# Loads of the last stage begun in the stage before it, and one gradient's stores issued by GpSimd, in a spectral layer's training step

## The chip, the cores and the metric

The kernel runs on one core of one Trainium2 chip. A core has TensorE (PE, matrix products), VectorE (DVE) and ScalarE (ACT) for elementwise work, GpSimd (POOL), and SyncE (SP), which in this kernel issues nearly every DMA. A DMA issued by any engine is moved by the core's 16 DMA engines. The metric is device time in microseconds (us), the median of several executions.

## The reference, cut to what matters

The program computes a conditioned layer (a spectral filter, then a dense pair with a squared relu) and all its gradients. With S = 2048 rows, D = 512 columns and F = 1792 hidden columns, all in bf16:

```
sa, ca, ga, sb, cb, gb = rows of silu(c) @ w_mod
h  = layernorm(x) * (1 + ca) + sa
x1 = x + ga * irfft2( rfft2(h) * (w_r + i w_i) )
h2 = layernorm(x1) * (1 + cb) + sb
out = x1 + gb * ( relu(h2 @ w1 + b1)**2 @ w2 + b2 )
outputs: out, then the gradients of sum(out * grad_out) by
         x, w_r, w_i, w1, b1, w2, b2, c, w_mod
```

out_0 is `out`, out_1 the gradient of x, out_2 and out_3 those of w_r and w_i (the spectral filter), out_4 of w1, out_5 of b1, out_6 of w2, out_7 of b2, out_8 of c, out_9 of w_mod.

## The kernel before, in words

The Fourier transforms are products with small cosine and sine matrices. Rows are held 128 to a tile column, 16 such row tiles (t = 0 to 15); the spectrum is held in eight groups (gi = 0 to 7) of 128 x 2 x 2 x 258.

The program goes forward (to about 130 us), through the dense pair forward and back (to about 282 us), and then has two stages that the change touches.

**The middle stage of the way back** (some 282 to 348 us, L1025 to L1135). `spec_f23` (L294) transforms the gradient of the spectral output, group by group: psB on PE (L318), two ACT copies into AE (L324, L325), psC on PE (L306), two ACT copies into G (L308), then `ew_b` (L1117): eight DVE products (L413 to L416) that give the gradient spectrum Z and the filter gradient gW, and the stores of gW to out_2 and out_3 (L1123; six stores for group 0, four for each other). `after_b` (L1125) follows each group: it loads later groups (`load`, L1107: LF from L1109, Z from L1110, X from L1112), loads LG (L1129), fills PE with units of the gradient of w1 (`grad_w1`, L1077, 16 products of 448 columns each, L1081, copied by ACT at L1085 and stored at L1087), and after every second group emits one row of the gradient of w_mod (`GMod.emit`, L447: a broadcast on PE at L452, an ACT copy into the single buffer gmbc at L454, then two wmc loads, L458, four DVE products with sums, L465, four scalings, L462 and L464, two stores, L467). Right after the second unit of `grad_w1` stands `grad_b1` (L1039), whose ACT copy b4 (L1047) is stored to out_5 (L1048). The units, grad_b1 and the broadcast of `emit` take their PSUM from one pool, `mmps`, of two buffers named "mm" in turn.

**The last stage** (some 348 us to the end). `spec_g1` (L331) transforms Z back over one axis (psG, L341, copied out by DVE at L346 and ACT at L348). Then `row_pair` (L1217) goes through the rows two tiles at a time: PE (L370, L380), an ACT copy (L1226), and some 15 DVE operations on the rows n1 and gxl, which `load_rows3` (L1167) loads two pairs ahead from HBM (L1170, L1171); L1231 is the first that reads n1, L1242 the one that reads gxl. Between the pairs PE is filled with 14 units of the gradient of w2 (`grad_w2`, L1147: 16 products of 512 columns, L1150, scaled by DVE at L1153, stored at L1154). A unit needs the whole output gradient g_sb (128 x 16 x 512, loaded at L1173) and one transposed chunk hn of the hidden activations (`load_hn`, L1141, a transposing DMA at L1145). Four hn buffers are loaded before the stage's work, four more in a pool `endp` that comes free when the units of grad_w1 end, and then in turn. `grad_b2` (L1157) and its second half (L1057 to L1065) stand among them.

**What sets the order.** A scheduler orders each engine's instructions by the order of the program text and by priorities when the program is built; on the chip each engine runs its own list strictly in order, SP's list of DMAs too, and waits where an operand, a buffer or a DMA's completion slot is not ready. DMAs from one issuing engine use eight completion slots in turn, so that an issue also waits for the one eight before it. A pool that is allocated over memory of a released pool waits for the last users of that memory: before the change, g_sb's pool `gwp` lies where the LF tiles and the tiles of `spec_f23` lay, so its load waits for the last stores of gW.

Of the kernel before, what the change touches and what calls it, by code (L numbers as in the profile page):

```python
# [12 lines left out]
BF16 = mybir.dt.bfloat16  # L13
# [5 lines left out]
D = 512  # L19
DF = 257  # L20
FP = 258
F = 1792
NFC = 14
NT = 16
# [3 lines left out]
P = 128  # L28
# [15 lines left out]
def w_parts(rows, gi):  # L44

    v = rows.rearrange("(q h g) f -> q h g f", h=2, g=16)
    if gi > 0:
        return [(0, 64, v[:, :, gi, :]), (64, 64, v[:, ::-1, 16 - gi, :])]
    c = rows.rearrange("(q c g) f -> q c g f", c=4, g=16)
    return [(0, 64, v[:, :, 0, :]), (64, 32, c[:, 0:2, 8, :]), (96, 32, c[:, 3:1:-1, 8, :])]  # L50
# [15 lines left out]
def build_basic(tc, constp):  # L66
    nc = tc.nc
    K = {}
    ident = constp.tile([P, P], BF16, name="ident")
    make_identity(nc, ident)  # L70
    K["ident"] = ident
    for nm, shape, dt, val in (("ones_sq", [P, P], BF16, 1.0), ("ones_col", [P, 1], BF16, 1.0), ("ones_q", [P, 32], BF16, 0.0), ("onef", [P, 1], FP32, 1.0),
                               ("nhalf", [P, 4], FP32, -0.5), ("npi", [P, 1], FP32, -math.pi), ("eps", [P, 1], FP32, 1e-5)):
        tl = constp.tile(shape, dt, name=nm)
        nc.vector.memset(tl, val)
        K[nm] = tl
    nc.vector.memset(K["ones_q"][:, 0:1], 1.0)
    pid = constp.tile([P, 1], I32, name="pid")
    nc.gpsimd.iota(pid, pattern=[[0, 1]], base=0, channel_multiplier=1)
    K["pid"] = pid  # L80
    pidf = constp.tile([P, 1], FP32, name="pidf")
    nc.vector.tensor_copy(pidf, pid)
    K["pidf"] = pidf
    return K
# [324 lines left out]
def cmul(nc, pool, A, B, outr, outi, conj_a):  # L409

    p1 = pool.tile([P, 2, 2, FP], BF16, name="p1")
    p2 = pool.tile([P, 2, 2, FP], BF16, name="p2")
    nc.vector.tensor_tensor(p1[:, :, :, 0:DF], A[:, :, :, 0:DF], B[:, :, :, 0:DF], op=ALU.mult)  # L413
    nc.vector.tensor_tensor(p2[:, :, :, 0:DF], A[:, :, :, 0:DF], B[:, :, ::-1, 0:DF], op=ALU.mult)  # L414
    nc.vector.tensor_tensor(outr, p1[:, :, 0, 0:DF], p1[:, :, 1, 0:DF], op=(ALU.add if conj_a else ALU.subtract))
    nc.vector.tensor_tensor(outi, p2[:, :, 0, 0:DF], p2[:, :, 1, 0:DF], op=(ALU.subtract if conj_a else ALU.add))  # L416
# [54 lines left out]
def kernel(  # L471
# [5 lines left out]
    nc = tc.nc  # L477
# [6 lines left out]
    xs_dram = dram.tile([P, 8, 2, 2, FP], BF16, name="xs_dram")  # L484
    h_dram = dram.tile([NFC, P, NT * P], BF16, name="h_dram")
# [6 lines left out]
    g_view = grad_out.rearrange("b (p t) d -> p (b t) d", t=NT)  # L492
# [20 lines left out]
    K = build_basic(tc, constp)  # L513
# [175 lines left out]
    with Priority(tc, LATE):  # L689
        for b in range(NB):  # L690
            for fc in range(NFC):
                ps = mmps.tile([P, SB], FP32, name="mm")
# [331 lines left out]


    gm = GMod(tc, K, scf, gsc, wm_view, out9_view)
    lf2 = tc.alloc_tile_pool(name="lf2", bufs=1, side="right")
    K["LF"] += [lf2.tile([P, 2, 3, P], BF16, name=f"LFb{gi}") for gi in range(4, 8)]
    W4 = 448
    NFB = F // W4  # L1030
    gwa = tc.alloc_tile_pool(name="gwa", bufs=1)
# [7 lines left out]
    def grad_b1():  # L1039

        ps = mmps.tile([P, SB], FP32, name="mm")
        for t in range(NT):
            for fb in range(NFB):
                nc.tensor.matmul(ps[32 * fb:32 * fb + 32, 0:W4], lhsT=K["ones_q"], rhs=ghn[t // 4][:, t % 4, fb * W4:(fb + 1) * W4],
                                 start=(t == 0), stop=(t == NT - 1), tile_position=(0, 32 * fb))
        b4 = gwa.tile([P, W4], BF16, name="b4", bufs=1)
        nc.scalar.copy(out=b4, in_=ps[:, 0:W4])  # L1047
        nc.sync.dma_start(out_5.rearrange("(q f) -> q f", q=NFB), b4[0:P:32, :])  # L1048

    def add_quadrants(ps, pool, out, scale=None):  # L1050
        w = ps.shape[-1]
# [38 lines left out]
    for fp in range(0, NFB, 2):  # L1090
        for dc in range(4):
            for fb in (fp, fp + 1):
                units.append(lambda fb=fb, dc=dc: grad_w1(fb, dc))
    units[1:2] = [lambda w1=units[1]: (w1(), grad_b1())]

    def fill_w1(n):
        for _ in range(n):
            if units:
                units.pop(0)()
# [4 lines left out]
    with tc.tile_pool(name="f23b", bufs=2) as fr, tc.tile_pool(name="ewb", bufs=2) as ew:  # L1104
        Xt = {}

        def load(gi):  # L1107
            if gi >= 4:
                nc.sync.dma_start(K["LF"][gi], LF_dram[:, 2 * gi:2 * gi + 2])  # L1109
            nc.sync.dma_start(Z[gi], wz_dram[:, gi])  # L1110
            Xt[gi] = fr.tile([P, 2, 2, FP], BF16, name="Xb", bufs=4)
            nc.sync.dma_start(Xt[gi], xs_dram[:, gi])  # L1112

        for gi in range(4):
            load(gi)

        def ew_b(gi, G):  # L1117
            cmul(nc, ew, Z[gi], G, Z[gi][:, :, 0, 0:DF], Z[gi][:, :, 1, 0:DF], True)
            gW = ew.tile([P, 2, 2, FP], BF16, name="gW", bufs=3)
            cmul(nc, ew, Xt[gi], G, gW[:, 0, :, 0:DF], gW[:, 1, :, 0:DF], True)  # L1120
            for i, o in enumerate((out_2, out_3)):
                for p0_, n, rows_ in w_parts(o, gi):
                    nc.sync.dma_start(rows_, gW[p0_:p0_ + n, i, :, 0:DF])  # L1123

        def after_b(gi):  # L1125
            if gi + 4 < 8:
                load(gi + 4)
            if gi == 4:
                nc.sync.dma_start(K["LG"], LG_dram)  # L1129
            fill_w1(2 if 0 < gi < 6 else 1)  # L1130
            if gi % 2 == 1:
                gms.pop(0)()

        spec_f23(tc, K, UT, AEs, None, lambda gi: gwa.tile([P, 2, 2, FP], BF16, name="G", bufs=2), ew_b, after_b)
    lf2.release()  # L1135
    gwp = tc.alloc_tile_pool(name="gwp", bufs=1, side="right")
    g_sb = gwp.tile([P, NT, D], BF16, name="g_sb")

    hns, endp = [], {}

    def load_hn():  # L1141
        fc = len(hns)
        if fc < NFC:
            hns.append(endp.get("hn", gwp).tile([P, NT, P], BF16, name="hn", bufs=4))
            nc.sync.dma_start(hns[fc], h_dram[fc, :, :], transpose=True)  # L1145

    def grad_w2(fc):  # L1147
        ps = mmps.tile([P, SB], FP32, name="mm")
        for t in range(NT):
            nc.tensor.matmul(ps, lhsT=hns[fc][:, t, :], rhs=g_sb[:, t, :], start=(t == 0), stop=(t == NT - 1))  # L1150
        gw = gwp.tile([P, D], BF16, name="gw", bufs=3)
        with tc.high_priority():
            nc.vector.tensor_tensor(gw, ps, modb[:, GB_B, :], op=ALU.mult)  # L1153
        nc.sync.dma_start(out6_view[:, fc, :], gw)  # L1154
        load_hn()
# [11 lines left out]
    def load_rows3(t):  # L1167
        if t < NT:
            rows3[t] = (fin.tile([P, 2, D], BF16, name="n1"), fin.tile([P, 2, D], BF16, name="gxl"))
            nc.sync.dma_start(rows3[t][0], n1_dram[:, t:t + 2, :])  # L1170
            nc.sync.dma_start(rows3[t][1], gx1_dram[:, t:t + 2, :])  # L1171

    nc.sync.dma_start(g_sb, g_view)  # L1173
    load_hn()
    load_rows3(0)
    load_rows3(2)
    for _ in range(3):
        load_hn()

    CS = utcs.tile([P, NT, 4, 16, 8], BF16, name="utcs")  # L1180
    spec_g1(tc, K, Z, CS)
# [100 lines left out]
    fp.release()  # L1282
    fin.release()
    gwp.release()
    h2p.release()
    cdp.release()
    cfp.release()
# [35 lines left out]
```

## Time and profile before

| what | value |
|---|---|
| median of 11 runs | 432.09 us (430.2 to 433.57) |
| the profiled execution | 435.41 us, of which its span (first to last instruction) is 433.6 us |
| granted TensorE clock, mean | 0.992 of full speed |
| busy share of the span | PE 92%, DVE 81%, ACT 60%, POOL 3% |
| 282 to 348 us: PE, DVE, ACT busy of 66 us | 63.13, 47.43, 35.02 us; DMA share 0.77, 228 GB/s |
| 348 to 432 us: PE, DVE, ACT busy of 84 us | 74.73, 70.49, 38.49 us; DMA share 0.99, 241 GB/s |
| gW stores (L1123) | 34 on SP, 591 ns to issue and 3.5 us to landing at the median |
| hn loads (L1145) | 14 on SP, 2905 ns to issue and 5.6 us to landing at the median |

How to read it: times are microseconds from the start of the span unless they are marked ns. "PE mm L1150" is TensorE's work at line 1150 that writes the tile "mm"; "SPq" is SP issuing a DMA; "n<-n_dram" is the tile n1 loaded from the tensor n1_dram, as buffer numbers are left out of names. A wait is named with the engine and line that waited, the arrow, and what ended the wait. The DMA share is the mean busy share of the 16 DMA engines. The chain that ended last is followed back from the last instruction, at each step to what released it.

### The profile page before, as it was taken

The numbers are of one execution on the slowest core, as the hardware profiler recorded it, in microseconds if no ns is written. First come the engines' busy times: TensorE is split into PE (matmuls) and PEld (weight loads), VectorE is DVE, ScalarE is ACT, GpSimd is POOL, SyncE is SP. The second block draws the span as 40 slices with busy tenths as digits, with TensorE's granted clock in tenths as the row PEclk, the third lists the DMA queues.
The fourth block names the chain that finished last, engine by engine and source line by source line (L and its number), as shares of the span: only waits on it lengthen the run. The fifth ranks groups of instructions, "written<-read, shape, count | busy, mean of one in ns | idle before, by whom it ended". The sixth has DMA issues, their size and how long they took to land.

```text
span 433.6 us, 7049 instructions
## 1 busy us (share of the span) xinstructions
PE 400.6 (92%) x2375; PEld 195.8 (45%) x2375; DVE 351.1 (81%) x846; ACT 261.2 (60%) x493; POOL 13.0 (3%) x64
## 2 busy tenths in 40 slices
PE   2798999999999999999999999999999799993996
PEld 0344456654434444444444344455565464441332
DVE  6797758958997588978897998929576968977996
ACT  4697889768882188248635855474348375445231
POOL 6210000000000000000000000000000000000000
PEclk9998999999999999999999999999999999999899
DMA  8995789989298569767965997987995699999994
GB/s 238 248 296 144 189 323 275 256 312 219 89 375 260 155 112 322 197 168 201 278 179 172 214 320 251 270 251 223 259 305 154 167 261 274 224 260 237 246 242 160
DMA packets 149738, 101.09 MB, mean 233 GB/s; under 512 B 98753, under 2 KB 135494, under 8 KB 149062
## 3 DMA queue, kind: packets, MB, share of 16 engines
q1 hardware_dynamic: 149138, 100.12, 86.1%
q10 hardware_dynamic: 564, 0.53, 0.4%
q8 instruction: 18, 0.29, 0.3%
q14 instruction: 18, 0.15, 0.1%
HBM read 35.44 MB, written 41.60 MB: 178 GB/s over the span
## 4 chain that ended last, share of the span: by engine, by line
PE 35%; DVE 31%; DMA 13%; ACT 10%; SPq 5%; issue 5%; POOL 1%; ACTq 0%; DVEq 0%
PE og L880 10%; PE mm L853 6%; PE mm L694 5%; PE mm L1150 4%; DMA n<-n_dram 3%; DVE gm_junk L465 3%; DMA x<-in_A_x_dram 2%; DMA LGb<-LG_dram 2%; PE psG L341 2%; PE mod_ps L595 2%; SPq L1145 2%; DVE l_st L795 1%; DVE jk L1235 1%; DMA gh_dram<-gab 1%; DVE p L414 1%
## 5 line engine op out<-in xcount | busy, mean ns | idle before, releaser
L694 PE MATMUL mm<-gT,w2T 128*128 128x512 bf16 x224 | 59.3, 390 | 2.7 <-DVE gab L697 2.3
L1150 PE MATMUL mm<-g_sb,hn 128*128 128x512 bf16 x224 | 51.7, 385 | 4.3 <-DVE gw L1153 4.3
L853 PE MATMUL mm<-h2T,w 128*128 128x512 bf16 x224 | 53.6, 379 | 1.5 <-ACT r L855 1.3
L880 PE MATMUL og<-w1T,gab 128*128 128x512 bf16 x224 | 50.9, 379 | 0.8 <-DVE o L945 0.7
L1081 PE MATMUL mm<-gab,h_sb 128*128 128x448 bf16 x256 | 51.4, 352 | 0.1
L880 PE MATMUL og<-w,h 128*128 128x512 bf16 x224 | 50.3, 379 | 0.0
L855 ACT ACTIVATE r<-mm,b1col 128x512 bf16<-128x512 f32 x56 | 37.0, 685 | 6.1 <-PE mm L853 3.7
L1150 PEld LDWEIGHTS <-hn 128*128 128x128 bf16 x224 | 21.3, 99 | 30.5 <-issue 7.6
L853 PEld LDWEIGHTS <-w 128*128 128x128 bf16 x224 | 21.1, 97 | 30.6 <-issue 8.8
L1081 PEld LDWEIGHTS <-h_sb 128*128 128x128 bf16 x256 | 24.6, 98 | 21.6 <-issue 1.0
L880 PEld LDWEIGHTS <-h 128*128 128x128 bf16 x224 | 21.8, 98 | 26.1 <-issue 1.0
L880 PEld LDWEIGHTS <-gab 128*128 128x128 bf16 x224 | 21.6, 98 | 25.9 <-issue 1.4
L694 PEld LDWEIGHTS <-w2T 128*128 128x128 bf16 x224 | 21.2, 100 | 23.5 <-issue 7.4
L893 ACT CAST G<-og 128x512 bf16<-128x512 f32 x16 | 9.2, 581 | 27.8 <-PE og L880 27.8
L699 ACT CAST gab<-mm 128x512 bf16<-128x512 f32 x36 | 21.7, 604 | 4.5 <-PE mm L694 4.4
L857 DVE TENSOR_TENSOR h<-r 128x1024 bf16<-128x1024 bf16 x28 | 19.1, 683 | 4.9 <-ACT r L855 4.9
L1230 ACT ACTIVATE gs<-gn,inv 128x512 bf16<-128x512 bf16 x16 | 11.4, 716 | 18.1 <-DVE gn L1228 18.1
L1085 ACT CAST gw<-mm 128x448 bf16<-128x448 f32 x16 | 8.7, 543 | 21.4 <-DMA out_dram<-gw 11.5
L413 DVE TENSOR_TENSOR p<-Z,G 128x1028 bf16<-128x1028 bf16 x8 | 5.6, 696 | 17.7 <-ACT G L308 9.4
L697 DVE CAST gab<-mm 128x512 bf16<-128x512 f32 x20 | 13.7, 686 | 7.5 <-PE mm L694 7.4
L372 ACT ACTIVATE Tsb<-psT 128x512 bf16<-128x512 f32 x32 | 18.5, 604 | 1.6 <-PE psT L370 1.6
L465 DVE SCALAR_TENSOR_TENSOR gm_junk<-wmc,onef,gmbc 128x512 bf16<-128x512 bf16 x24 | 17.9, 744 | 1.6 <-ACT gmbc L454 0.7
(287 smaller groups left out, 756.4 us busy)
## 6 DMA issues: line engine op xcount, KB each, us to landing
h_dram<-h SPq DMA_DIRECT2D x28, 256.0 KB, 3.2
gh_dram<-gab SPq DMA_DIRECT2D x28, 256.0 KB, 3.5
w<-in_B_w_dram SPq DMA_DIRECT2D x2, 1792.0 KB, 7.6
wmc<-in_w_mod_dram SPq DMA_DIRECT2D x12, 256.0 KB, 4.4
out_dram<-gwm SPq DMA_DIRECT2D x12, 256.0 KB, 3.4
wz_dram<-Z SPq DMA_DIRECT2D x8, 258.0 KB, 2.4
xs_dram<-Xs SPq DMA_DIRECT2D x8, 258.0 KB, 3.6
Z<-wz_dram SPq DMA_DIRECT2D x8, 258.0 KB, 4.2
```

Of the source, the lines that this page charges most:

```text
L372: nc.scalar.activation(Tsb, ps, AF.Copy, scale=EF_S)
L465: nc.vector.scalar_tensor_tensor(out=junk, in0=wmc[:, i, :], scalar=K["onef"], in1=gmbc, op0=ALU.mult, op1=ALU.mult, accum_out=self.gsc[:, ...
L694: nc.tensor.matmul(ps, lhsT=w2T[:, dc, fc * P:(fc + 1) * P], rhs=gT[b][:, :, dc, :], start=(dc == 0), stop=(dc == 3))
L697: nc.vector.tensor_copy(out=gaT[b][:, fc, :], in_=ps)
L699: nc.scalar.copy(out=gaT[b][:, fc, :], in_=ps)
L853: nc.tensor.matmul(ps, lhsT=w1[:, dc, (fc + i) * P:(fc + i + 1) * P], rhs=h2T[b][:, :, dc, :], start=(dc == 0), stop=(dc == 3))
L855: nc.scalar.activation(r[:, i, :], ps, AF.Relu, bias=b1col[:, fc + i:fc + i + 1])
L857: nc.vector.tensor_tensor(h2, r, r, op=ALU.mult)
L880: nc.tensor.matmul(ps, lhsT=lhs(fc), rhs=rhs[:, fc, :], start=(fc == 0), stop=(fc == NFC - 1))
L1081: nc.tensor.matmul(ps[:, 0:W4], lhsT=h2_sb[:, t, dc * P:(dc + 1) * P], rhs=ghn[t // 4][:, t % 4, fs], start=(t == 0), stop=(t == NT - 1))
L1150: nc.tensor.matmul(ps, lhsT=hns[fc][:, t, :], rhs=g_sb[:, t, :], start=(t == 0), stop=(t == NT - 1))
L1230: nc.scalar.activation(gs[:, i, :], gn[:, i, :], AF.Copy, scale=inv1[:, t + i:t + i + 1], accum_out=rr[:, i, 0:1])
```

## The change

Three things change, all from L1026 on.

- g_sb and two hn buffers move into a pool of their own, `gsp`, which is allocated ahead of the LF tiles, so that it overlaps nothing of the middle stage. g_sb's load is issued in `after_b` of group 4, behind LG; hn 0 and hn 1 are issued in `after_b` of groups 4 and 5, each not ahead of the last X load. At the start of the last stage only hn 2 and hn 3 are loaded, from a `gwp` that now has two hn buffers.
- The stores of gW (34) and of b4 (one) are issued by GpSimd's queue instead of SP's.
- b4 of grad_b1 has no buffer of its own any more: it is written into the pool's one buffer "gmbc", which `GMod.emit` uses next.

In the built program, the order on PE and on DVE is the same as before. On ACT the first half of a copy into AE (L324) now stands before the first gmbc copy, and the second half (L325) directly behind it. On SP, the LF loads of groups 4 to 7, which stood ahead of the first Z, stand behind the first four pairs of Z and X. On GpSimd's queue stand, in order: six gW stores of group 0, four of group 1, the store of out_5, then four for each of groups 2 to 7. hn 2 waits for the last eight of these to land, and the loads of n1 and gxl follow it on SP.

The diff, cut to its core:

```diff
     gm = GMod(tc, K, scf, gsc, wm_view, out9_view)
+    gsp = tc.alloc_tile_pool(name="gsp", bufs=1, side="right")
+    g_sb = gsp.tile([P, NT, D], BF16, name="g_sb")
+    hns, endp = [], {}
+
+    def load_hn():
+        fc = len(hns)
+        if fc < NFC:
+            pool = gsp if fc < 2 else endp.get("hn", endp["gw"])
+            hns.append(pool.tile([P, NT, P], BF16, name="hn", bufs=4 if "hn" in endp else 2))
+            nc.sync.dma_start(hns[fc], h_dram[fc, :, :], transpose=True)
...
-        b4 = gwa.tile([P, W4], BF16, name="b4", bufs=1)
-        nc.scalar.copy(out=b4, in_=ps[:, 0:W4])
-        nc.sync.dma_start(out_5.rearrange("(q f) -> q f", q=NFB), b4[0:P:32, :])
+        b4 = gwa.tile([P, D], BF16, name="gmbc", bufs=1)
+        nc.scalar.copy(out=b4[:, 0:W4], in_=ps[:, 0:W4])
+        nc.gpsimd.dma_start(out_5.rearrange("(q f) -> q f", q=NFB), b4[0:P:32, 0:W4])
...
             Xt[gi] = fr.tile([P, 2, 2, FP], BF16, name="Xb", bufs=4)
-            nc.sync.dma_start(Xt[gi], xs_dram[:, gi])
+            K["Xt"] = nc.sync.dma_start(Xt[gi], xs_dram[:, gi]).ins
...
                 for p0_, n, rows_ in w_parts(o, gi):
-                    nc.sync.dma_start(rows_, gW[p0_:p0_ + n, i, :, 0:DF])
+                    nc.gpsimd.dma_start(rows_, gW[p0_:p0_ + n, i, :, 0:DF])
...
             if gi == 4:
                 nc.sync.dma_start(K["LG"], LG_dram)
+                nc.sync.dma_start(g_sb, g_view)
+            if 4 <= gi < 6:
+                with tc.issue_after(K["Xt"]):
+                    load_hn()
             fill_w1(2 if 0 < gi < 6 else 1)
...
     gwp = tc.alloc_tile_pool(name="gwp", bufs=1, side="right")
-    g_sb = gwp.tile([P, NT, D], BF16, name="g_sb")
-
-    hns, endp = [], {}
-
-    def load_hn():
-        fc = len(hns)
-        if fc < NFC:
-            hns.append(endp.get("hn", gwp).tile([P, NT, P], BF16, name="hn", bufs=4))
-            nc.sync.dma_start(hns[fc], h_dram[fc, :, :], transpose=True)
+
+    endp["gw"] = gwp
...
-    nc.sync.dma_start(g_sb, g_view)
     load_hn()
     load_rows3(0)
     load_rows3(2)
-    for _ in range(3):
-        load_hn()
+    load_hn()
```

More of the change, by code (lines that the diff above doesn't have):

```diff
@@ L1284 @@
     gwp.release()
+    gsp.release()
     h2p.release()
```

## The prediction

> **What bounds the kernel now.** I read the slices of the page first. PE shows 9 in nearly every slice of the whole way back (from 282 us on), so a microsecond is won only where PE stands still, and lost only where it is made to. Then I asked what PE waited for from 280 us to the end (line, releaser, us in total, times, longest):
>
> ```profile
> PE mm L1150 <- DVE gw L1153: 4.3, 1, 4.3
> PE mm L1060 <- DVE gn L1239: 2.6, 1, 2.6
> PE psG L341 <- DVE utcs L346: 2.1, 1, 2.1
> PE mm L1277 <- DVE gcb L1275: 0.5, 1, 0.5
> PE psB L318 <- ACT AE L325: 0.3, 1, 0.3
> ```
>
> Nothing else is over 0.3. The table of 4 us stretches places the first two (PE, PEld, DVE, ACT, POOL busy, then clock, DMA share, GB/s); the clock falls once, behind the second wait:
>
> ```profile
> 392.00:396.00 4.00, 1.52 (x13) 0.64 (x14) 4.00 (x12) 2.43 (x5) 0.00 (x0) 1.00 1.24 247
> 396.00:400.00 4.00, 0.28 (x5) 0.16 (x3) 1.75 (x4) 2.67 (x7) 0.00 (x0) 1.00 0.83 198
> 400.00:404.00 4.00, 3.46 (x10) 0.96 (x10) 4.00 (x12) 1.36 (x3) 0.00 (x0) 0.57 1.09 313
> ```
>
> Behind both stands DVE, and behind DVE the n1 rows of the last stage. From DVE's waits (from 345 us on):
>
> ```profile
> DVE q L1231 <- DMA n<-n_dram: 6.0, 3, 2.3
> ```
>
> From the chain that ended last (start, length):
>
> ```profile
> 385.50 3.69 DMA n<-n_dram
> 394.63 4.54 DMA n<-n_dram
> ```
>
> And from SP's timeline (start, length of the issue):
>
> ```profile
> 348.71 7.01 SPq L1145 DMA_TRANSPOSE hn<-h_dram  x1
> 380.18 5.22 SPq L1145 DMA_TRANSPOSE hn<-h_dram  x2
> 389.96 4.57 SPq L1145 DMA_TRANSPOSE hn<-h_dram  x1
> ```
>
> The reader is to see that each n1 load is issued in the very microsecond in which a transposed h load lets go of SP (355.7, 385.4, 394.5). The transposes are slow to issue (7.0 us at worst, 2.0 at best, median 2.9) since the DMA engines are full: their share is 0.99 of the stretch 348 to 432, and 0.77 of 282 to 348.
>
> **Part 1, the moved loads.** g_sb (2048 KB) and two of 14 hn loads go from 348-366 to some 308-325. DVE's three waits for n1 (1.5, 2.3, 2.3 us) should go: n1 of the first rows then has one transpose ahead of it in place of g_sb and a 7 us one; at 380-395 the engines have less to carry. g_sb's 2 MB at 241 GB/s (that stretch's rate) is 8.5 us of them, the two hn some 4 us each (estimate: landing 4.8 to 10.6, partly overlapped), 16 of 83 busy us. PE order and DVE order are the same instruction for instruction in both programs, so the waits can be followed one by one. L1060 waits behind DVE work that comes 1.5 + 2.3 = 3.8 us sooner: the wait of 2.6 goes. L1150 is then reached 2.6 sooner, at 393.7, and its releaser, gw L1153 (399.8 to 400.5), 6.1 sooner, at 394.4: 0.7 of 4.3 is left, 3.6 are won. The clock's dip goes with it: four matmuls took 1.87 where four take 0.9 warm, and the next dozen 3.04 in place of 2.76: 1.3. What is late next is gw L1153 itself; from 404 PE has no idle time but the last 0.5. **Part 1: 2.6 + 3.6 + 1.3 = 7.5 won.** If the n1 loads stay late it is nothing; never more than the 6.9 of idle plus 1.3, so 0 to 8.2.
>
> What these loads do in the middle stage: SP issues LFb4 to 7 behind the first four Z and Xb pairs instead of before (their first reader, psC of group 4, comes at 314.7); LGb moves from 313.5 to about 303; hn0 (about 319) and hn1 (about 323) come ahead of two wmc loads that DVE wants at 332.3, with 4.2 us landing. A full set of DMA engines there (0.77 x 66 = 51 busy us, 67 with the guests) could make wmc late and so group 6's products and psG's wait of 2.1 longer. Against that, ACT's L1085 waited 6.4 us at 325.7 for a store that stood behind SP's other work and now goes out at about 316; DVE's group 5 began late for it (328.5). Bounds: 2.1 won to 3 lost (a wmc landing as late as the worst Xb, 6.8, behind a slow hn1). I take 0.4 won.
>
> **Part 2, the stores on GpSimd's queue.** SP loses 34 gW issues of 0.6 us and the b4 store: 21 us of SP time, none of it on PE's path, so free by itself. But POOL has them in order, and there is a new wait. grad_b1's b4 now shares the one gmbc buffer, so ACT's first gmbc copy (L454) must wait until out_5 has landed, and out_5 stands on POOL behind all ten stores of groups 0 and 1. Behind that copy on ACT are the second half of AE, two gwm scalings, G and gw1. And PE waits for it: the two "mm" buffers rotate, so the second of the two grad_w1 units begun at 300.40 writes the buffer that this copy empties. Today:
>
> ```profile
> 299.26 0.59 ACT L454 CAST gmbc<-mm 128x512 bf16<-128x512 f32 x1
> 300.40 6.21 PE L1081 MATMUL mm<-gab,h_sb 128*128 128x448 bf16 x32
> 296.17 4.05 SPq L1123 DMA_DIRECT2D out_dram<-gW  x6
> 301.26 2.50 SPq L1123 DMA_DIRECT2D out_dram<-gW  x4
> 305.46 0.64 SPq L1048 DMA_DIRECT2D out_dram<-b  x1
> ```
>
> That second unit begins at 300.40 + 6.21/2 = 303.5. The stores can begin when DVE has group 0's gW, at 296.1; 0.7 sooner, since Xb (which DVE waited for, 8.4 us) follows an out_0 store that took 3.64 beside LFb loads and 2.4 at the median. With c us per store on POOL, out_5 is issued at 295.4 + 10c, lands 3.0 later (the 32-row gW stores' median), and the copy takes 0.6: PE stands from 303.5 to 299.0 + 10c, that is **10c - 4.5 us**. c is shown nowhere: no DMA of this kernel is issued by POOL. From below, SP's own 0.6 for the same store gives 1.5 us; from above, POOL's longest instruction, 128x4 at L401 (1064 ns), 6.1, and a third more (c = 1.4, since ten stores may bring waits for earlier ones' landing) 9.5. A c under 0.45 would cost nothing; a gain is excluded, as out_5 has no reader. I take 0.9: it is the same kind of instruction as SP's row, on the engine of the other, and I lean to the engine: 4.5 us. A gap of that size came with the dip above (1.3) once, gaps of 2.1 and 2.6 did not; I count half, 0.7. **Part 2: 5.2 lost**, 1.5 to 10.8 at the ends.
>
> A rule bears on c. The Trainium skill, "DMA: Bandwidth & Descriptors" (section "Latency and other measured facts"), gives GpSimd's path about 1 us to the first byte, where SP's has 0.6; taken as c, that would make the stall 5.5 and the sum 1.0 worse. No run shown here has it. It speaks against the change, as does a trap in "SBUF — State Buffer" (section "SBUF: two separate sides"): VectorE in a two-port mode keeps GpSimd from writing its descriptors; no row here can show that.
>
> At the seam both effects meet: hn2 and all n1 loads wait for the last gW stores. DVE has gW of group 7 at 343.2; eight stores from 339.1 at 0.9 end at 346.4, landed by 349.4. SP then needs 2.9 for hn2 and n1 4.0: 356.3. It is wanted at 358.8, so free up to c = 1.2.
>
> **Sum.** 7.5 + 0.4 - 5.2 = 2.7 us won. The profiled execution took 435.41 (span 433.6), 0.8% over the median of 432.09, so I subtract from the median: **429.4 us**.
>
> **Rivals.**
> 1. *The new wait wins.* One mechanism, one place: ACT at L454, price 10c - 4.5 + 1.3, against 7.9 won; it decides from c = 1.11. At c = 1.4 it is 10.8 - 7.9 = 2.9 lost: 435.0. For: ten stores in a row in front of one tiny store. Against: SP does them in 0.6. Chance 0.27.
> 2. *The tail keeps its waits.* n1 of rows 10 still stands behind hn8 on SP, and the crowded middle costs 1 or 2: say 3 won in all and 5.2 lost, 434.3. For: the order on SP there is the same pair as before. Against: hn8's buffer is free from 382.5, so only full DMA engines hold it up. Chance 0.13.
> 3. *GpSimd issues as fast as SP* (c = 0.6): 7.9 - 1.5 = 6.4 won, 425.7. For: 34 stores of few bytes. Against: POOL's 1064 ns for four columns. Chance 0.15.
> 4. *It does not do what it says*: the stores stay SP's bound and the seam is as late as before (gW of group 7 is made at 343.2 in either program). Then only the two hn's time is won, 3 to 4, against 5: within 2 of today. Contained in the first two.
> The forecast, with c from 0.75 to 1.05, has 0.45; a small part of it, and of case 2, lies within 0.2% (0.9 us, about what a measurement of this kernel can tell from no change): 0.11 in all. So faster 0.49, slower 0.40. As both signs hold much, the forecast's own range is 427.0 to 431.5. The whole: case 3 with the largest gains (432.1 - 8.2 - 2.1 + 1.5 = 423.3) to case 1 with a crowded middle (432.1 - 7.5 + 3 + 10.8 = 438.4); cut by the ends that need two extremes at once, 424.5 to 438.
>
> **What would show it.** Right: SP's n1 loads follow hn issues of 3 us or less, DVE's L1231 has no wait left, PE no idle 4 us near 390; ACT waits for a DMA at its first gmbc copy near 300, PE at 303.5 for ACT, 3 to 6 us, and POOL's eleven stores show c. Wrong: no wait at that copy (out_5 landed by 303), a clock dip near 305-310 with over 7 us of it, DVE waiting for wmc or n1, or psG's wait grown past 3 us.

## The result and the profile after

The changed kernel takes 438.14 us (median of 12 runs, 436.35 to 440.13) where the kernel before took 432.49 beside it: a ratio of 1.0132 (95% interval 1.0108 to 1.0156), 5.65 us slower. The forecast was 429.4. The profiled execution has a span of 436.7 us and a mean clock of 0.988.

Lines have moved: the matmuls of the gradient of w1 are L1092 (L1081 before), their copy and store L1096 and L1098 (L1085, L1087), the row sums of the gradient of b1 and their copy and store L1055, L1058 and L1059, the gW stores L1134, the hn loads L1036, the matmuls of the gradient of w2 and their scaling L1158 and L1161 (L1150, L1153). What PE waits for from 280 us to the end (line, releaser, us in total, times, longest):

```profile
PE mm L1092 <- ACT gmbc L454: 7.8, 1, 7.8
PE psG L341 <- DVE utcs L346: 2.3, 1, 2.3
PE mm L1158 <- DVE gw L1161: 1.4, 1, 1.4
PE mm L1283 <- DVE gcb L1281: 0.5, 1, 0.5
PE psF L354 <- DVE Z L415: 0.5, 1, 0.5
```

The wait of 2.6 at the row work is gone and that of 4.3 at the gradient of w2 is down to 1.4; a new one of 7.8 stands at the place that the prediction named. The same table of stretches as before (PE, PEld, DVE, ACT, POOL busy, clock, DMA share, GB/s):

```profile
300.00:304.00 4.00, 2.28 (x13) 1.08 (x11) 0.00 (x0) 0.00 (x0) 1.77 (x3) 1.00 1.07 323
304.00:308.00 4.00, 0.00 (x0) 0.00 (x0) 0.00 (x0) 0.00 (x0) 0.00 (x0) 0.56 0.99 400
308.00:312.00 4.00, 1.95 (x6) 0.82 (x6) 1.97 (x7) 2.59 (x5) 0.00 (x0) 0.50 0.11 46
...
400.00:404.00 4.00, 3.40 (x23) 1.39 (x22) 4.00 (x11) 1.39 (x4) 0.00 (x0) 1.00 1.00 230
```

From 304 to 308 no engine computes at all while the DMA engines move 400 GB/s, and the clock is at half (0.56, then 0.50) until 312. The stretch that had a clock of 0.57 before (400 to 404) keeps it whole. Who holds PE is read along three timelines (start, length, what, and in brackets the idle time before it and who ended it). GpSimd's:

```profile
294.57 4.67 POOL L1134 DMA_DIRECT2D out_dram<-gW  x8 [40.80 <-PE mm L1055]
300.99 1.17 POOL L1134 DMA_DIRECT2D out_dram<-gW  x2 [1.76 <-DMA out_dram<-gW]
302.15 0.60 POOL L1059 DMA_DIRECT2D out_dram<-gmbc  x1
```

ACT's, then PE's:

```profile
309.41 0.59 ACT L454 CAST gmbc<-mm 128x512 bf16<-128x512 f32 x1 [10.20 <-DMA out_dram<-gmbc]
```

```profile
299.10 3.19 PE L1092 MATMUL mm<-gab,h_sb 128*128 128x448 bf16 x16
310.05 5.49 PE L1092 MATMUL mm<-gab,h_sb 128*128 128x448 bf16 x16 [7.76 <-ACT gmbc L454]
```

Eight gW stores go out in 4.67 us, 0.58 each; the ninth then waits 1.76 for a completion slot, that is for the first of them to land; out_5 is issued at 302.15 and lands 7.2 us later. PE's next unit takes 5.49 us where a warm one takes 3.19: another 2.3. Just ahead of out_5, SP had issued LG (1.5 MB), which it issued at 313.52 in the kernel before:

```profile
300.11 0.99 SPq L1140 DMA_DIRECT2D LGb<-LG_dram  x1
```

In the last stage the moved loads did what they were to do. SP's timeline shows hn 0 and hn 1 in the middle stage, with an out_4 store between them, and n1 behind one short hn:

```profile
326.52 6.17 SPq L1036 DMA_TRANSPOSE hn<-h_dram  x1
332.79 0.53 SPq L1098 DMA_DIRECT2D out_dram<-gw  x1
333.37 5.12 SPq L1036 DMA_TRANSPOSE hn<-h_dram  x1
338.54 1.10 SPq L458 DMA_DIRECT2D wmc<-in_w_mod_dram  x2
...
358.77 1.89 SPq L1036 DMA_TRANSPOSE hn<-h_dram  x1
360.71 0.58 SPq L1178 DMA_DIRECT2D n<-n_dram  x1
```

No wait of DVE for n1 is left. DVE's waits of the middle stage show what the two transposes did instead, ahead of wmc:

```profile
DVE gm_junk L465 <- DMA wmc<-in_w_mod_dram: 4.1, 1, 4.1
```

**Three marks on PE** split the way back so that single runs can be compared: the first matmul of the row sums (the start of "L1044" below), before which PE has the same work in every version; the first matmul of the gradient of w2, with which the last stage's fill begins; and the last matmul. From the views of these lines (count, ns at least/at the median/at most, first and last start in us), before and after:

```profile
L1044 PE MATMUL mm<-gab,ones_q x64: 352/352/363, 292.5 to 295.3; 128*32 128x448 bf16 x64
L1150 PE MATMUL mm<-g_sb,hn x224: 379/379/631, 361.0 to 429.2; 128*128 128x512 bf16 x112
L1277 PE MATMUL mm<-ident,gcb x1: 218/218/218, 430.1 to 430.1; 128*4 128x128 bf16 x1
```

```profile
L1055 PE MATMUL mm<-gab,ones_q x64: 352/352/363, 291.2 to 294.0; 128*32 128x448 bf16 x64
L1158 PE MATMUL mm<-g_sb,hn x224: 376/379/390, 371.0 to 432.5; 128*128 128x512 bf16 x112
L1283 PE MATMUL mm<-ident,gcb x1: 218/218/218, 433.4 to 433.4; 128*4 128x128 bf16 x1
```

So the **middle** took 361.0 - 292.5 = 68.5 us and takes 79.8; the **tail** took 69.1 and takes 62.4. 6.7 won, 11.3 lost (7.8 in which PE stands idle, 2.3 of clock, 0.7 more at psG and psF): 4.6 slower in the two profiled executions, 5.65 in the medians. The first mark itself lies between 290.8 and 293.9 in the profiles of this study, so a single profile says nothing finer than some 1.5 us about a total.

### The profile page after: what moved, and what is told of

The parts are those of the page before. It is cut to its first block, busy times and chain, and to the rows that moved or that the text cites. A ratio compares the mean times of both kernels' runs of the same rounds, so it can differ in the third digit from the quotient of the medians.

```text
span 436.7 us, 7064 instructions
## 1 busy us (share of the span) xinstructions
PE 399.5 (91%) x2375; PEld 195.0 (45%) x2375; DVE 351.0 (80%) x846; ACT 261.0 (60%) x493; POOL 33.5 (8%) x99
## 4 chain that ended last, share of the span: by engine, by line
PE 45%; DVE 25%; ACT 11%; DMA 9%; issue 4%; SPq 3%; POOL 1%; ACTq 0%; DVEq 0%; POOLq 0%
PE og L880 11%; PE mm L853 9%; PE mm L694 5%; PE mm L1092 4%; PE mm L1158 3%; PE psG L341 3%; SPq L1036 3%; DVE gm_junk L465 3%; DMA out_dram<-gW 2%; PE mod_ps L595 2%; DMA out_dram<-gmbc 2%; DMA n_dram<-x_sb 2%; ACT AE L324 1%; DVE gw L1161 1%; DMA out_dram<-gx 1%
## 5 line engine op out<-in xcount | busy, mean ns | idle before, releaser
L1092 PE MATMUL mm<-gab,h_sb 128*128 128x448 bf16 x256 | 53.7, 363 | 7.8 <-ACT gmbc L454 7.8
L694 PE MATMUL mm<-gT,w2T 128*128 128x512 bf16 x224 | 57.2, 379 | 3.2 <-DVE gab L697 2.6
L1158 PE MATMUL mm<-g_sb,hn 128*128 128x512 bf16 x224 | 50.5, 379 | 1.4 <-DVE gw L1161 1.4
L1092 PEld LDWEIGHTS <-h_sb 128*128 128x128 bf16 x256 | 25.2, 100 | 30.9 <-issue 11.5
L1158 PEld LDWEIGHTS <-hn 128*128 128x128 bf16 x224 | 21.1, 98 | 27.2 <-issue 3.8
L1134 POOL DMA_DIRECT2D out_dram<-gW x34 | 19.9, 598 | 81.3 <-PE mm L1055 40.8
L1096 ACT CAST gw<-mm 128x448 bf16<-128x448 f32 x16 | 8.6, 540 | 20.8 <-PE mm L1092 14.1
L861 DVE TENSOR_TENSOR gab<-r,gab 128x1024 bf16<-128x1024 bf16 x28 | 19.1, 681 | 0.0
```

The costliest lines, as they stand in the source:

```text
L694: nc.tensor.matmul(ps, lhsT=w2T[:, dc, fc * P:(fc + 1) * P], rhs=gT[b][:, :, dc, :], start=(dc == 0), stop=(dc == 3))
L861: K["gh"] = nc.vector.tensor_tensor(gh, r, gh, op=ALU.mult).ins
L1092: nc.tensor.matmul(ps[:, 0:W4], lhsT=h2_sb[:, t, dc * P:(dc + 1) * P], rhs=ghn[t // 4][:, t % 4, fs], start=(t == 0), stop=(t == NT - 1))
L1134: nc.gpsimd.dma_start(rows_, gW[p0_:p0_ + n, i, :, 0:DF])
```

## The experiments

Theory 1: the buffer that b4 shares with gmbc is the loss, and the moved loads win what was forecast. Theory 2: the moved loads crowd the middle stage, and the stand is only where that shows. All runs, by the ratio to the kernel before (95% interval) and, from one profile each, middle and tail as above:

| run | what it is | ratio | middle | tail |
|---|---|---|---|---|
| | before | 1 | 68.5 | 69.1 |
| | the change | 1.0132 (1.0108 to 1.0156) | 79.8 | 62.4 |
| e3 | stores on GpSimd alone | 0.9983 (0.9949 to 1.0017) | 66.6 | 69.9 |
| e4 | moved loads alone | 1.0048 (1.0012 to 1.0083) | 73.6 | 65.0 |
| e5 | shared buffer alone | 1.0111 (1.0068 to 1.0154) | 74.4 | 69.4 |
| e1 | the change, own b4 | 0.9937 (0.9893 to 0.9982) | 70.7 | 62.4 |
| e2 | the change, out_5 on SP | 1.0032 (0.9999 to 1.0066) | 75.4 | 64.5 |
| e10 | the change, out_5 on ACT | 0.9908 (0.9873 to 0.9943) | 70.9 | 62.4 |
| e6 | the change, LG and g_sb held | 1.0043 (1.0007 to 1.0078) | 79.8 | 62.4 |
| e7 | e1, g_sb held | 1.0047 (1.0015 to 1.0079) | 77.3 | 64.5 |
| e8 | e1, hn behind wmc | 0.9877 (0.9818 to 0.9936) | 72.9 | 62.4 |
| e9 | e1, one out_4 store earlier | 0.9929 (0.9906 to 0.9951) | 72.9 | 62.4 |
| e11 | e8 and e9 together | 0.9873 (0.9821 to 0.9924) | 68.5 | 62.3 |

The kernel before itself took 432 to 437 us on the chips used, so ratios are compared and not times.

**The three parts apart (e1, e3, e4, e5).** e1 gives b4 a place of its own (modulation rows that nobody reads any more); all else is as changed:

```
-        b4 = gwa.tile([P, D], BF16, name="gmbc", bufs=1)
+        b4 = modb[:, SB_B, :]
```

> The changed kernel with one thing undone: the bias gradient's row sums go into a tile of their own (the space of modulation rows that nobody reads any more) and no longer into gmbc's buffer; out_5 and gW are still stored from GpSimd. Theory 1 (the shared buffer is the loss): ScalarE's copy at L454 waits for nothing, TensorE's 7.8 us stand at L1092 and the slow 2.3 us behind it go, and the moved loads' gain stays: 438.1 - 10 = 428 us, between 426.5 and 430. Theory 2 (the moved loads crowd the middle stage, and the stand at L1092 is only where it shows): the copy is on time but TensorE stands at psG and psF instead, and at most half comes back: 433 us or more.

Measured: 430.36 us beside 433.49, and once more on another chip:

> The version with a tile of its own for the row sums once more, on the chip of the two that follow: 430.4 us was its time in a first look, 2.7 us under the kernel before; the same ratio, 0.99, within half a per cent.

433.11 beside 436.31: 0.9924 (0.9891 to 0.9958). PE's waits in the profile of e1's first run, which is also the one in the table:

```profile
PE mm L1092 <- ACT gw L1096: 2.3, 1, 2.3
PE mm L1158 <- DVE gw L1161: 1.4, 1, 1.4
PE mm L1283 <- DVE gcb L1281: 0.5, 1, 0.5
PE psG L341 <- DVE utcs L346: 0.5, 1, 0.5
```

The 7.8 are gone, and the ratio falls from 1.0132 to 0.993, some 2%, 8 to 9 us: Theory 1 for the sign of the change, with 428 forecast and 430.4 found. What is left, another stand at L1092, is taken up below. The other parts alone, first the stores on GpSimd (`nc.gpsimd` in place of `nc.sync` at the gW and out_5 stores of the kernel before):

> The kernel before with only the gW and out_5 stores moved to GpSimd's queue (row sums in their own tile, loads not moved). Theory 1: nothing waits for these stores, the last stage's waits at L1060 and L1150 stay: 432 us, within 1.5 of the kernel before. Rival (stores on GpSimd cost VectorE or the middle stage something by themselves): 434 us or more.

432.91 us: no difference that can be measured, with waits at L1060 (4.4) and L1150 (0.7) still in the last stage. So GpSimd's issuing the stores costs nothing by itself that this run can tell (the interval ends 0.2% above 1). The moved loads alone (the change with own b4, gW and out_5 on `nc.sync`):

> The moved loads alone: grad_out and two h loads begun in the middle stage, gW and out_5 stored from SyncE as before, the row sums in a tile of their own. Theory 1: the 6.5 to 7.5 us that the last stage won are kept and nothing is paid for them: 425 to 427 us. Theory 2 (crowding): SyncE's queue, which now holds the gW stores as well as the moved loads, brings spectrum or wmc loads later, and TensorE's stands at psG and psF grow by 3 us or more: 429 us or more.

434.8 us, half a per cent slower: here Theory 2 was right in the total, but not in the place. PE's stand at psG is 2.4 us as before; with the gW stores and the moved loads both on SP's queue PE stands 3.3 us for ACT at L1092, and 3.2 at its last product where it was 0.5. The tail wins 4.1 and the middle loses 5.1. The two edits belong together: the loads win only with the stores off SP's queue. The shared buffer alone (b4 in gmbc's buffer, all stores on SP):

> The kernel before with one thing added: the row sums of the bias gradient go into gmbc's buffer; all stores stay on SyncE, no load is moved. Theory 1 (the shared buffer is the loss by itself, wherever its store is issued): out_5 is issued behind two groups of gW stores near 304 us and lands some 3 to 5 us later, so L454's copy comes near 308 us instead of near 301 and TensorE stands 4 to 8 us at the filter-gradient unit behind it: 437 to 442 us. Theory 2 (the moved loads are what makes the landing late): out_5 lands within 3 us and the loss stays under 4 us: 434 to 436 us.

441.95 beside 436.76, 4.8 us lost at a ratio of 1.0111, without any moved load. So the shared buffer costs by itself. PE's loss is not the 4 to 8 in one place that was expected: 2.1 at L1081 with 1.7 of lower clock behind it, and 2.6 at psG.

**Why out_5 lands so late (e2, e6, e10).** Either the DMA engines are full whichever queue a store comes from (1a), or GpSimd's queue is slow (1b). e2 issues out_5 from SP, in the shared buffer (`nc.sync.dma_start(out_5...`):

> The changed kernel with the 3.5 KB store of out_5 back on SyncE's queue, in the shared gmbc buffer all the same; the gW stores stay on GpSimd. Theory 1a (the store lands late because the 16 DMA engines are full of the spectrum loads and of LG, whichever queue it comes from): it lands 5 us or more after its issue, TensorE still stands 5 us or more, 435 us or more. Theory 1b (a store from GpSimd's queue lands late by itself, and GpSimd's wait for a free completion slot adds 1.8 us): out_5 lands within 4 us of an issue before 300 us, TensorE stands under 3 us, 430 to 432 us. If the queue order of SyncE itself brings the issue behind several loads, the landing time tells the two apart, not the total.

435.22 us: as 1a has it in the time. Issued at 300.72, it let ACT go at 306.11: 5.4 us, as 1a has it too. But PE stood only 2.3 us for that copy, where 1a had 5 or more; the profiled execution took 438.85, above the median. e6 leaves out_5 on GpSimd but keeps LG and g_sb off the engines until L454's copy is through, behind the first out_9 store on SP (kept as `K["o9"]`):

```
-                nc.sync.dma_start(K["LG"], LG_dram)
-                nc.sync.dma_start(g_sb, g_view)
+                with tc.issue_after(K["o9"]):
+                    nc.sync.dma_start(K["LG"], LG_dram)
+                    nc.sync.dma_start(g_sb, g_view)
```

> The changed kernel with LG and grad_out held back on SyncE's queue until the first out_9 store, which itself waits for the copy at L454; everything else as changed, the shared buffer and out_5 on GpSimd too. Theory 1a (LG, 1.5 MB issued 2 us ahead of out_5, keeps the DMA engines full): out_5 lands 4 us after its issue or sooner instead of 7.2, TensorE's stand at L1092 falls from 7.8 to 4 us or less, 433 to 435 us. Theory 1b (the spectrum loads issued ahead of it, or GpSimd's own queue, hold it up): landing and stand stay within 1 us of the changed kernel's, 437 to 439 us, or more where LG then comes late for the stage that needs it.

From its DMA table (KB, us from issue to landing):

```profile
out_dram<-gmbc POOLq DMA_DIRECT2D x1, 3.5 KB, 4.5
```

4.5 in place of 7.2, from the same queue, with the DMA share at 0.50 in place of 0.90 between issue and landing: what the engines carry changes the landing, as 1a has it. But in this execution GpSimd began its stores 2.1 us later (296.64), so that PE still stood 6.4 us; the stand of 4 or less that 1a forecast was not found. The total is 0.9% under the change's, while the two profiles have the same middle and tail; I leave the total open. e10 issues the store from ACT, right behind the copy that fills it, and keeps the shared buffer (`nc.scalar.dma_start(out_5...`):

> The changed kernel with the out_5 store issued from ScalarE's own queue right behind the copy that fills it; the shared buffer stays. In the changed kernel 7.2 us passed between that copy and the issue on GpSimd, behind ten gW stores, and 7.2 us more until it landed. Theory 1a (the engines are full, so a store lands late from any queue): issue near 295 us, landing 5 to 7 us later, L454's copy near 301.5 us, TensorE's stand at L1092 0 to 1.5 us, 429 to 431 us, and the two halves of the loss are told apart. Theory 1b (it is GpSimd's queue that lands late): landing within 3.5 us, no stand at all, 428 to 429 us.

432.5 beside 436.31, as good as e1. ACT's timeline:

```profile
296.14 0.63 ACTq L1059 DMA_DIRECT2D out_dram<-gmbc  x1
...
301.31 0.59 ACT L454 CAST gmbc<-mm 128x512 bf16<-128x512 f32 x1 [2.96 <-DMA out_dram<-gmbc]
```

5.2 us from issue to the copy, on a queue with nothing ahead: 1a again (the 3.5 of 1b falls). What no run tells for certain is whether GpSimd's queue adds something. With the engines nearly full (a share of 0.90 to 1.04) the store took 3.4 to 5.4 us from SP and ACT (e5, e10, e2) and 6.1 to 9.5 from GpSimd; but all of the latter were issued behind LG and none of the former was. Stores of SP behind LG and g_sb were late too: 10.2 us for one of out_4 (e1), up to 8.9 for gW (e4). The loss of the change is told apart: of the 14.5 us between b4's copy (done at 294.9) and L454's (309.4), 7.2 are the way to the issue behind ten stores and their slots, and 7.2 the landing. e10 took away 6.3 of the first and 2.0 of the second, and of PE's stand for L454's copy nothing is left.

**What the moved loads do cost in the middle (e7, e8, e9, e11).** e1's middle is 4.1 us longer than e3's. Its ACT stood for an out_4 store, the second, which empties the buffer that the copy at L1096 writes; SP had issued that store behind an Xb load whose buffer was not yet free (ACT's timeline, then SP's):

```profile
316.08 0.53 ACT L1096 CAST gw<-mm 128x448 bf16<-128x448 f32 x1 [5.93 <-DMA out_dram<-gw]
```

```profile
305.10 0.34 SPq L1123 DMA_DIRECT2D Xb<-xs_dram  x1
305.53 0.40 SPq L1098 DMA_DIRECT2D out_dram<-gw  x1
305.99 1.29 SPq L458 DMA_DIRECT2D wmc<-in_w_mod_dram  x2
307.32 1.13 SPq L1141 DMA_DIRECT2D g_sb<-in_grad_out_dram  x1
```

First guess: g_sb's 2 MB, issued 1.8 us behind it, makes it late. e7 holds g_sb (and with it hn 0 and hn 1) until the out_9 stores of the second modulation row:

> The version with a tile of its own for the row sums, and grad_out and the two h loads held back until the out_9 stores of the second modulation block (near 318 us instead of 307). In the version without the hold, ScalarE's copy of the filter gradient stood 5.9 us for an out_4 store that was issued 2 us ahead of the 2 MB load, and TensorE 2.3 us for ScalarE, with some 1.7 us of lower clock behind it. Theory 2b (the early 2 MB load is what makes that store late): the stand and the dip go, 430.4 - 4 = 426.4 us, if the two transposed loads, now later, hold up nothing else. Rival (LG and the spectrum loads alone fill the engines at that time): the stand stays, 430 us; or it moves to the out_4 store between the two transposed loads, 430 us or more.

438.82 beside 436.76: the guess falls. g_sb was issued at 324.65, and the store still took 11.0 us to land, the stand was 3.5; and the held transposes came worse (hn 0 took 9.2 us of SP's time, ACT stood a second time for a store behind it, and DVE 7.3 us for wmc). e8 puts hn 0 and hn 1 behind the wmc loads of the third row (no `load_hn()` in `after_b`, three at the start of the last stage, which the scheduler draws forward to there), e9 the second out_4 store ahead of the out_9 stores and of that Xb (`tc.high_priority()` around this one store):

> The version with a tile of its own for the row sums, with the two wmc loads of the third modulation block ahead of the two transposed h loads on SyncE's queue; grad_out as early as in the change. Theory 1: without the shared buffer's delay VectorE did not wait for wmc any more, so the order costs and wins nothing: 430.4 us, within 1. Theory 2 (the transposed loads, 5.5 and 3.6 us of SyncE's time, are what crowds the middle stage): 428 us or less.

> The same version with one store moved on SyncE's queue: the second out_4 store right behind LG, ahead of the out_9 stores and of the Xb load that stood some 3 us for its buffer. Theory 3 (ScalarE's stand of 5.9 us there came from this store's issue behind the standing Xb load and from its landing of 10.2 us behind LG): the store is issued some 2.5 us sooner, but lands behind LG all the same, so ScalarE's stand falls to 3.5 us or less and TensorE's 2.3 us and the 1.7 us of lower clock go: 426 to 427 us. Rival (the engines are so full that the store lands at the same time whenever it is issued): 430 us.

e8's ratio is 0.9877, e1's 0.9937 and 0.9924, with intervals that overlap: no clear difference, and in its profile PE still stands 3.2 us for the second out_4 store. e9 removed the stand it was aimed at: the store is issued at 304.75, 2.1 us behind LG, and the copy that needs its buffer starts at 314.93 behind PE and waits for no store. So Theory 3 is right about the place; how long that store took to land the trace does not give. Yet e9 won nothing (0.9929): its waits show the next ones, at psG and, at L1093, for an out_4 store between the two transposes:

```profile
PE psG L342 <- DVE utcs L347: 2.3, 1, 2.3
PE mm L1093 <- ACT gw L1097: 1.7, 1, 1.7
```

Both together:

> The version with a tile of its own for the row sums, the second out_4 store right behind LG, and the two transposed h loads behind the wmc loads of the third modulation block. Theory 3 (what is left of the middle stage's loss is two out_4 stores that land late, one behind LG and a standing Xb load, one between the two transposed loads): neither ScalarE stand reaches TensorE any more, the middle stage takes 67 to 69 us from the row sums to the first matmul of the last stage, as with the stores on GpSimd alone, and the last stage 62.4: 1.3 to 1.6 per cent under the kernel before. Rival (the stand only moves on to the next buffer): 0.7 to 0.9 per cent under it, as with each alone.

429.14 beside 435.93: 0.9873, some 5.5 us under the kernel before, and the lowest ratio here, beside e8's, which cannot be told from it. Its middle and tail (68.5 and 62.3) are those that were expected; the ratio is at the edge of the expected one. PE's longest waits from 250 us on:

```profile
PE psG L342 <- ACT utcs L349: 1.5, 1, 1.5
PE mm L1157 <- DVE gw L1160: 1.4, 1, 1.4
PE psG L342 <- DVE utcs L347: 0.9, 1, 0.9
```

No stand for ACT in the units of grad_w1 is left. That its middle equals the one before (68.5) and not e3's (66.6) leaves 1.9 us of the moved loads' cost. Nearly all of it stands at psG, where PE waits 2.4 us and in e3 0.7; what makes psG late is open.

## Why the prediction was wrong

- *Part 1, the tail: right.* 7.5 forecast, 6.7 measured. The L1060 wait is gone as forecast, the clock's dip is gone, DVE's waits for n1 too; of the 4.3 at the gradient of w2 1.4 are left and not 0.7.
- *Part 1, the middle: wrong in sign.* 0.4 won was taken; e1 against e3 shows some 4 us lost (single profiles), and by the ratios the moved loads win about 0.5% with the stores on GpSimd where 6.7 us would be 1.5%. The named risk (hn ahead of wmc) was one half; the other half, an out_4 store behind a standing Xb load, was not seen. e11 shows both by removing them. In the change itself little of this shows beside the long stand: without the stand and the clock its middle is 1.2 longer than before.
- *Part 2, the cost c of a store on GpSimd: over-estimated, and not what decided.* 0.9 was taken, 0.59 is the median of 34, and SP's was 0.59. With 10c - 4.5 the stand would have been 1.4. The 3.1 too much hid, by luck, half of what the next line has too little.
- *Part 2, "lands 3.0 later": the step that failed.* The landing was taken from four stores of the kernel before, issued between 296 and 300, where the DMA share was 0.53; in the change it is 0.99 to 1.07 between 296 and 308, and the store took 7.2, that is 4.2 more. The wait for a completion slot, counted only at the upper end, added 1.8. Together 6.0 us, which turns 1.4 into 7.4; 7.8 were measured. The prediction itself had read the full engines as the reason for slow transposes, and had LG brought forward to about 303; it did not use either for the store. The mechanism and its place were right: the wait of ACT's copy for out_5 was mis-sized.
- *The clock: half a dip of 1.3 (0.7) was counted, and 2.3 came.*
- *The sum.* From 2.7 won to 4.6 lost in the two profiles are 7.3: 3.3 of the stand (7.8 for 4.5), 1.6 of the clock, 1.6 of the rest of the middle (1.2 lost for 0.4 won), 0.8 of the tail. The medians have 1.0 more, which no view explains.
- *The seam: right.* hn 2 took SP 1.89 us, n1 was never late.
- *Rival 1 is what happened, by place and by consequence*, but its price came from the landing, not from c; its point of decision (c = 1.11) was set on the wrong quantity.
- *The rule on GpSimd's 1 us to the first byte*, taken as the cost of an issue, did not show: 34 stores were issued at the pace of SP's. The first byte itself is in no row. Nor is VectorE seen to keep GpSimd from issuing: the eight stores of 294.57 to 299.24 went at 0.58 each while DVE was busy 3.4 of the 5 us (in which mode, the trace does not tell), and out_5 took its 7.2 us while DVE did nothing (0.00 from 300 to 308). What the Trainium skill says in "DMA: Bandwidth & Descriptors", section "Issuing engines are not separate DMA queues", fits what the runs show: transfers of all issuers go over the same 16 engines and interleave, and moving them to another queue saves issue time only. That rule, read beside the DMA share, would have warned of the landing.

## What to carry to other kernels

Before a buffer is shared with one that is being stored, add up the way of that store from its issue to its landing in the stretch where it will stand: every store ahead of it on its queue, its completion slot, and a landing time found where the DMA engines are as full, not the median of the kernel. When loads are drawn forward, look at what small transfer on the same queue now stands behind them, since a 3.5 KB or 224 KB store that frees a buffer of the bottleneck can cost more than the megabytes that pass it. A part that wins only beside another one (here the loads, once the stores are off SP) must be tried with it.

## What the runs showed of the hardware

- The same 3.5 KB store landed 3.4 us after its issue (SP, e5), 4.5 (GpSimd, e6), 5.2 (ACT, e10), 5.4 (SP, e2), 6.1 (GpSimd, e3), 7.2 (GpSimd, the change), 7.9 (e1) and 9.5 (e7). The same queue gave the best but one and the worst: 4.5 at a DMA share of 0.50, 9.5 at 1.03. But the share alone does not set it: at 1.03 and 1.04 ACT's and SP's stores took 5.2 and 5.4. The four longest were all issued behind LG, the four shortest were not.
- A stand of PE lowered the clock or not at nearly the same length. The 16 to 32 matmuls behind it took 1.7 us too long after 2.1, 2.3 and 3.5 us (e5, e1, e7; clock 0.53, 0.59 and 0.68 in the 2.6 to 3.4 us behind), 2.9 after 3.2 (e8), 2.6 after 6.4 (e6) and 2.3 after 7.8 (the change), but nothing after another 2.3 (e2) and another 2.9 (e7), with the clock at 1.00. The Trainium skill, "TensorE: Matmul & The Clock Gate" (section "What's actually happening"), has the clock fall after an idle window of about 3.4 us; here stands of 2.1 us were enough in some cases, and the measurement decides. The loss does not grow in step with the stand.
